# A gated state-space convolution and feed-forward mix on one core: the same steps in another written order

## The chip, the cores and the metric

The kernel runs on one core of one Trainium2 chip. A core has a matrix engine (TensorE, PE in the profile, its weight loads PEld), a vector engine (VectorE, DVE), an engine for functions and scaled copies (ScalarE, ACT), GpSimd (POOL) and SyncE (SP), which here only issues transfers. Each engine takes its instructions strictly in the order in which they were written, and waits on semaphores for what the others made. Matmul results stand in PSUM, everything else in SBUF. The metric is device time in microseconds, the median of three runs; lower is better.

## What is computed

The reference, cut to its core. `x` is 2048 rows of 640, `N` is 128, `F` is 1728:

```python
g = sigmoid((x * gate_w).sum(-1, keepdims=True))
# a: a long convolution of x along the rows, one kernel K for each of 640 columns
P = exp((dt * A)[:, :, None] * arange(L))
K = einsum("dn,dnl,dn->dl", C, P, dt * B).real
a = irfft(rfft(pad(x.T)) * rfft(pad(K))).T + x * Dskip
# b: a gated feed-forward block
b = (gelu(x @ w_gate) * (x @ w_up)) @ w_down
return g * a + (1 - g) * b
```

## The kernel before

Everything is cut into named steps. A dictionary holds for each name a small function that issues one or a few instructions. At the end a loop goes through the words of the table `ORDER` and calls them one after the other; the order in the table is the order on every engine's queue. What follows a slash in a word is either the PSUM buffer of a matmul group (0 to 3; there are four, of two banks each) or the engine of an eviction (A for ACT, D for DVE). Nothing else decides the order.

The names that the text uses, with `.0` and `.1` for the two halves of 320 of the 640 columns in the tables, and of 1024 rows in the feed-forward part:

- `lp0` to `lp5`: loads of the six parameter matrices (A_re, A_im, C_re, C_im, B_re, B_im; line 265); `t0` to `t5` turn them on PE (L297); `al` (L319), `al2` and `th` (L322) are decay and phase on DVE; `c2`, `c3` copy two turned ones on ACT (L326); `v0` to `v18` compute a square root and an angle from them, on DVE and ACT in turn.
- `xa`, `xb`: exponentials on ACT (L447, L449, L457, L461), single (320 wide) and double (640); `tabE`, `tabT`, `tabG`: loads of ACT's function tables.
- `fa`, `fb`: phases on DVE (L469, L477, L464); `sa`, `sb`: their sines on ACT (L481, L487); `ma`, `pa`, `pb`, `pc`: products on DVE (L492, L496, L505). When all of one half are there, `ct` contracts them on PE (L517, L518) in six blocks of 24 matmuls and one of 16, and `ek` copies each block out, in two instructions (L381 or L383). `ks` adds the skip term, `kd` and `kt` send the result out and back in another layout. `oa` and `ob` are memsets on POOL (L545, L546).
- `g`, `u`, `h`: gate and up projections on PE (L376), ten matmuls of 512 each; `eg`, `eu` evict them, `sg`, `su` spill what is kept in DRAM. `lw`, `x`: loads of weights and of the transposed input. `gl`: 80 small matmuls for the gate `g`. For late parts `dg` and `du` evict with the gelu and the product at once.
- `uf`: folds of the input (L367), each from a plain load `ul` and two gathers `ur` on POOL (L360). `us` stores a fold, `lu` loads a part of it.
- `rl`, `rg`: loads of spilled parts; `ge`: gelu on ACT; `hm`: up times gelu on DVE (L682). The loads `rl` share a ring of three slots.
- `U`, `K`: the two transforms on PE (L693, L706), `eU`, `eK` their evictions; `m`, `s`, `y`: products and sums in the frequency domain on DVE (L748 to L755); `I`: the inverse (L766), `eI`; `D`: down projection (28 matmuls, L781); `Z`: the mix (L788, L789); `o` evicts, `st` stores.

The written order runs in stages that overlap: parameters and exponentials (to about 31 us), the first half's tables beside the projections of the first 1024 rows (to 74), the first contraction (74.7 to 80.7), the second half's exponentials (to 98), its tables beside the second rows' projections (to 141), the second contraction, transforms and gelu (to about 184), and products, inverses, down projections and stores to the end.

Of the kernel before, what the change touches and what calls it, by code (L numbers as in the profile page):

```python
# [50 lines left out]
sa4.0 g11.0/0 eg11.0/A sa3.0 lw6 g12.0/1 eg12.0/A su8.0 su9.0 x4.1 us1 su7.0 pa4.0 fa6.0 leu1 ul2 sa6.0 pa3.0 fa5.0
g10.0/3 eg10.0/A sa5.0 pa6.0 ma5.0 pa5.0 u11.0/2 eu11.0/A u10.0/0 u12.0/1 ur2 eu10.0/A ct0.2/3 ct0.1/2 ct0.4/0
eu12.0/A ek0.4/A fb0.1 uf2.0 ek0.2/D uf2.1 ct0.0/1 ct0.6/3 ek0.6/D ek0.1/A ct0.3/0 ct0.5/2 ek0.3/D ek0.0/D ek0.5/D
ks.0 lw7 su10.0 su11.0 h.0/3 eg13.0/D ul3 su12.0 us2 ob.1 ur3 tabE2 xa11.1 xb11.1 xb3.1 xb21.1 xa17.1 xb19.1 xa9.1
xa15.1 xa16.1 eu13.0/D uf3.0 ma5.1 lw8 h.1/0 oa.1 xa7.1 xb23.1 g12.1/1 xa3.1 xa14.1 xa10.1 ma3.1 eg12.1/D xb5.1 xb27.1
xb1.1 xb17.1 xa19.1 xb14.1 xb10.1 xb13.1 xb4.1 xb7.1 xb31.1 xb25.1 xb9.1 xa8.1 xb6.1 xb12.1 xb2.1 xb8.1 xa4.1 xb29.1
xa1.1 xa5.1 xb15.1 tabT2 sb0.1 u12.1/2 eu12.1/D su13.0 eg13.1/D sg13.1 sg12.1 leu3 su12.1 uf3.1 ma2.1 u0.1/3 eu0.1/D
ma6.1 g0.1/1 g1.1/2 kd.0 lw9 eu13.1/A gl/3 gl1 ma4.1 fb1.1 ma1.1 eg0.1/D sg0.1 su0.1 lfm ma0.1 us3 sb1.1 u1.1/1 g2.1/0
lw10 su13.1 fb2.1 pb0.1 pc0.1 pb1.1 pc1.1 sb2.1 U000/3 eg2.1/A eU000/A fb4.1 pb2.1 pc2.1 eg1.1/A eu1.1/A fb3.1 fil.1
sb4.1 sg2.1 u2.1/0 sg1.1 eu2.1/A su1.1 lkm fa0.1 pb4.1 pc4.1 sb3.1 g3.1/3 U001/2 eU001/A u3.1/1 eg3.1/A u4.1/0 U003/2  # L60
fb5.1 pb3.1 pc3.1 lw11 su2.1 sg3.1 sa0.1 pa0.1 fa2.1 g4.1/3 eu3.1/A eU003/A sb5.1 eg4.1/A eu4.1/A su3.1 sa2.1 U002/1
g5.1/2 pb5.1 fa1.1 fa4.1 pa2.1 eg5.1/A sa1.1 u5.1/3 g6.1/0 kt.0 su4.1 sg4.1 eu5.1/A eg6.1/A sg5.1 pa1.1 fa3.1 sa4.1
u6.1/2 eu6.1/A su5.1 sg6.1 lwd0 su6.1 lu01 u7.1/3 K000/0 sa3.1 fa6.1 pa4.1 pa3.1 fa5.1 eU002/A K001/2 eK001/A g7.1/1
K011 eK011/D eu7.1/A sa6.1 eg7.1/D pa6.1 sa5.1 K002/3 K003/2 eK002/A K012 eK003/A K013 pa5.1 eK000/A eK012/A K010
ct1.4/1 ct1.5/3 lw12 lw13 su7.1 rl0.0 tabG sg7.1 eK013/D m0001 ek1.4/D ek1.5/D eK010/A ge1.0 gl2 ct1.2/2 ct1.1/0
ek1.1/A ek1.2/A ct1.3/1 hm0.0 rl3.0 rg3.1 ct1.6/3 ct1.0/0 rl1.0 lkm2 rl2.0 ek1.3/D m0100 ek1.6/A U012/2 eU012/A U013/1
eU013/A U010/3 U011/2 m0000 y000 ek1.0/A ks.1 eU010/D ge3.0 eU011/A gl3 m0110 y001 s0100 hm1.0 g8.1/1 g9.1/0 u9.1/3
K022/2 dg8 ge12.0 dg9 ge13.0 gf/1 gf1 ge9.0 ge5.0 g10.1/0 lu03 kd.1 du9 hm3.0 hm2.0 m0111 m0101 eK022/A K021/1 u8.1/3
g11.1/2 s0101 dg10 u10.1/0 pm0/A ge7.0 ge11.0 dg11 eK021/A rg1.1 rl4.0 hm4.0 lim rl6.0 rg6.1 rl5.0 lu02 er0 rl7.0 du8
y011 hm6.0 hm5.0 rg7.1 rg0.1 rl9.0 rl8.0 du10 y010 u11.1/3 K023/2 eK023/A U033/1 eU033/A hm7.0 du11 U022/0 eU022/A  # L70
U020/2 eU020/A hz0 hz1 lwz0 lwz1 U021/1 eU021/A rl10.0 er1 U023/0 eU023/A K031/3 eK031/A rg5.1 lu10 U031/2 U032/1
eU032/A eU031/A I001/0 K032/3 eI001/A eK032/A I000/1 eI000/A m0211 hm8.0 rl11.0 hm10.0 K033/2 U100/0 eK033/A U030/3
eU100/A eU030/A U103/1 U101/2 eU101/A U102/0 eU102/A eU103/A K020/3 eK020/A I011/2 K030/0 eK030/A m0220 hm9.0 rl13.0
lwe0 m0210 hm11.0 rl12.0 ge1.1 s0220 hm12.0 hm13.0 m0221 s0221 rg4.1 rg2.1 rl0.1 rg13.1 ge13.1 er2 rl1.1 kt.1 lu11
m0200 hm1.1 hm0.1 s0200 m0201 I010/1 m0300 eI010/A s0201 y021 m0310 ge5.1 rl4.1 lu12 rg12.1 rl2.1 D000/3 Z000 o000/A
# [789 lines left out]
```

## Time and profile before

| | us |
|---|---|
| median of 3 runs | 290.28 |
| the three runs | 290.28, 289.33, 291.79 |
| the profiled execution | 288.91 |
| its span, first to last instruction | 287.1 |
| PE, DVE, ACT busy | 264.5, 261.8, 222.7 |

The mean granted clock of the matrix engine was 0.988 of full speed. In the rows of the timeline that are shown, the first number is the start in microseconds from the span's start and the second the duration; then engine, line, operation, what it writes and reads, how many, and in brackets the idle time of the engine ahead of it with what ended it. "SPq" and "POOL" rows on transfers give the time of issuing, not that of the transfer. Matmuls overlap in the array, so the time between starts counts, not the duration of one.

### The profile page before, as it was taken

How to read it: one execution, taken by the hardware profiler on the slowest of the kernel's cores; microseconds unless marked ns; L12 is line 12 of the kernel's file. 1: busy time of each engine (PE TensorE's matmuls, PEld its weight loads, DVE VectorE, ACT ScalarE, POOL GpSimd, SP SyncE). 2: the span in 40 equal slices, each digit the busy share in tenths (PEclk: the TensorE clock that was granted, in tenths of full speed). 3: DMA queues.
4: the chain of work that ended last, by engine and by line, in shares of the span. 5: the costliest groups of instructions: out<-in, count | busy, mean ns of one | idle time of the engine just before them, and what ended most of it. 6: DMA issues, size and time to landing. Idle time of an engine off the chain costs nothing.

```text
span 287.1 us, 4933 instructions
## 1 busy us (share of the span) xinstructions
PE 264.5 (92%) x1883; PEld 159.8 (56%) x1883; DVE 261.8 (91%) x336; ACT 222.7 (78%) x324; POOL 14.1 (5%) x23
## 2 busy tenths in 40 slices
PE   3899799999999699998799998999999999999974
PEld 1744344444754434444584455777777767777753
DVE  1689999999998898999999999999999999999960
ACT  4699999799899978999999988999856545313320
POOL 2202000030040000000010000000000000000000
PEclk9999999999999969999999999999999999999999
DMA  7992479979382897858948877782355000010001
GB/s 200 221 227 75 136 223 272 213 182 304 101 265 66 193 321 220 301 186 263 332 117 222 278 200 215 225 256 67 95 142 162 25 23 23 25 46 25 23 23 46
DMA packets 63148, 46.94 MB, mean 163 GB/s; under 512 B 23275, under 2 KB 53526, under 8 KB 62998
## 3 DMA queue, kind: packets, MB, share of 16 engines
q1 hardware_dynamic: 62166, 44.90, 55.4%
q0 software_dynamic: 384, 1.31, 1.6%
q10 hardware_dynamic: 576, 0.43, 0.5%
q8 instruction: 14, 0.23, 0.3%
q14 instruction: 8, 0.07, 0.1%
HBM read 29.39 MB, written 14.62 MB: 153 GB/s over the span
## 4 chain that ended last, share of the span: by engine, by line
PE 36%; DVE 32%; ACT 17%; DMA 8%; issue 4%; SPq 2%; POOL 0%; DVEq 0%; ACTq 0%
PE ps L376 15%; DVE work L751 8%; DVE work L752 8%; PE ps L781 7%; DVE work L748 5%; PE ps L693 4%; ACT tail L481 3%; DMA work<-PMd 3%; PE ps L766 2%; ACT work L381 2%; ACT tail L487 2%; PE ps L706 2%; DVE work L383 2%; PE ps L517 2%; DMA tail<-PMd 2%
## 5 line engine op out<-in xcount | busy, mean ns | idle before, releaser
L376 PE MATMUL ps<-xT,Wr 128*128 128x512 bf16 x540 | 122.1, 385 | 7.1 <-DVE work L383 3.2
L376 PEld LDWEIGHTS <-Wr 128*128 128x128 bf16 x540 | 53.3, 99 | 72.4 <-issue 12.5
L381 ACT CAST work<-ps 128x640 bf16<-128x640 f32 (+2 forms) x59 | 47.8, 842 | 14.2 <-PE ps L766 7.5
L387 ACT ACTIVATE Wr<-ps,gs 128x320 bf16<-128x320 f32 x29 | 13.7, 524 | 29.4 <-issue 16.4
L752 DVE TENSOR_TENSOR work<-work 128x2560 bf16<-128x2560 bf16 x24 | 35.8, 1490 | 0.7
L781 PE MATMUL ps<-xT,work 128*128 128x320 bf16 x224 | 31.7, 299 | 0.0
L781 PE MATMUL ps<-xT,H 128*128 128x320 bf16 x224 | 31.6, 299 | 0.0
L481 ACT ACTIVATE tail<-work 128x1920 bf16<-128x1920 int16 x14 | 25.7, 1854 | 1.8 <-DVE work L464 1.7
L781 PEld LDWEIGHTS <-H 128*128 128x128 bf16 x224 | 21.9, 98 | 8.5
L781 PEld LDWEIGHTS <-work 128*128 128x128 bf16 x224 | 21.9, 98 | 8.5
L505 DVE TENSOR_TENSOR work<-tail,work 128x1920 bf16<-128x1920 bf16 (+1 forms) x22 | 23.1, 1090 | 0.0
L487 ACT ACTIVATE tail<-work 128x960 bf16<-128x960 int16 (+1 forms) x24 | 20.8, 926 | 0.8 <-DVE work L505 0.8
L766 PE MATMUL ps<-work,tail 128*128 128x320 bf16 x128 | 19.5, 299 | 1.8 <-DVE work L754 1.8
L469 DVE SCALAR_TENSOR_TENSOR work<-tail 128x320 int32<-128x320 f32 x42 | 18.0, 483 | 0.9 <-ACT tail L487 0.5
L464 DVE TENSOR_SCALAR work<-work 128x960 int32<-128x960 int16 (+1 forms) x26 | 16.5, 634 | 1.3
L766 PEld LDWEIGHTS <-tail 128*128 128x128 bf16 x128 | 12.4, 98 | 7.4 <-issue 2.2
L693 PEld LDWEIGHTS <-early 128*128 128x128 bf16 x128 | 12.4, 98 | 7.1 <-DMA tail<-PMd 1.7
L706 PE MATMUL ps<-KTt,early 128*128 128x320 bf16 x80 | 15.0, 299 | 1.4 <-ACT early L387 1.2
L496 DVE TENSOR_TENSOR work<-tail,work 128x1920 bf16<-128x1920 bf16 x14 | 15.9, 1151 | 0.3 <-ACT tail L481 0.3
L383 DVE CAST work<-ps 128x1024 bf16<-128x1024 f32 (+2 forms) x11 | 12.4, 1146 | 2.6 <-PE ps L766 1.6
L457 ACT ACTIVATE work<-tail 128x320 bf16<-128x320 f32 x30 | 12.5, 454 | 1.4 <-DVE tail L319 1.4
L693 PE MATMUL ps<-work,early 128*128 128x320 bf16 x80 | 13.1, 299 | 0.0
(119 smaller groups left out, 405.6 us busy)
## 6 DMA issues: line engine op xcount, KB each, us to landing
Ud<-work SPq DMA_DIRECT2D x22, 256.0 KB
work<-Ud SPq DMA_DIRECT2D x22, 256.0 KB
Wr<-in_B_w_gate_dram SPq DMA_DIRECT2D x12, 320.0 KB
Wr<-in_B_w_up_dram SPq DMA_DIRECT2D x12, 320.0 KB
PMd<-early SPq DMA_DIRECT2D x4, 640.0 KB
Gd<-work SPq DMA_DIRECT2D x9, 256.0 KB
work<-Gd SPq DMA_DIRECT2D x9, 256.0 KB
out_dram<-Wr SPq DMA_DIRECT2D x14, 160.0 KB
```

The source lines that it names most:

```text
L376: P.matmul(t[:, x, :], lhsT=Wr[:, slot, kt, cols:cols + 128], rhs=xT[:, th, kt, 512 * x:512 * x + 512], start=(kt == 0), stop=(kt == 4))
L381: A.copy(out=out, in_=in_)
L383: V.tensor_copy(out=out, in_=in_)
L481: act(out=T, in_=low16(t)[:, :, :, ::2], func=ACT.Sin, scale=SIN_SCALE)
L487: act(out=o[:, r], in_=i[:, r], func=ACT.Sin, scale=SIN_SCALE)
L505: tt(out=B2[:, :, :, cols].rearrange("p r g x -> p g r x"), in0=Tv if hf == 0 else Tv[:, :, ::-1], in1=e, op=ALU.mult)
L693: P.matmul(t[:, r, 0:W2], lhsT=FM[:, e, r, 128 * m:128 * m + 128], rhs=pm[:, r, e], start=(e == 0), stop=(e == 1))
L706: P.matmul(t[:, r, 0:W2], lhsT=mat[:, r, 128 * m:128 * m + 128], rhs=KTt[:, q, d], start=(x == 0 and j != 1), stop=(x == len(seq) - 1), sk ...
L751: step(f"m{h}{c}{i}{part}", lambda ux=ux, kx=kx: tt(out=fl(t), in0=ux, in1=kx, op=ALU.mult))
L752: step(f"s{h}{c}{i}{part}", lambda dst=dst, op=op: tt(out=fl(dst), in0=fl(dst), in1=fl(t), op=op))
L766: P.matmul(t[:, r, 0:W2], lhsT=IM[:, m, r, 128 * e:128 * e + 128], rhs=Y[:, r, m], start=(m == 0), stop=(m == 3))
L781: P.matmul(t[:, x, 0:W2], lhsT=H[c // 2][:, ft, tk:tk + 128], rhs=at[f"Wd{h}"][:, ft], start=(ft == 0), stop=False)
```

## The change

Only the table `ORDER` differs. The 875 words name the same steps; nearly every one stands in another place. The search that had made the first table was carried on, with the figures it works with unchanged. 17 words change the engine of an eviction, and many the PSUM buffer of a matmul group. The first line of the table, of before and of after:

```diff
-ldt leu2 lp3 one oa.0 idx sk ob.0 lp0 lpk tdt/0 t0/1 tabE dt al xb27.0 al2 xa4.0 xb14.0 xb17.0 xb4.0 xb8.0 xa1.0
+lp0 lpk ldt one tdt/0 t0/1 tabE dt al xb21.0 oa.0 sk al2 xb5.0 hz0 idx leu2 lp1 t1/2 xb1.0 xb19.0 xb25.0 xa8.0 xb3.0
```

The words that change engine, in the order of before:

| from DVE to ACT | from ACT to DVE |
|---|---|
| `eg2.0`, `ek0.2`, `eg0.1`, `eg7.1`, `ek1.4`, `ek1.5`, `ek1.3`, `o121` | `eu12.0`, `ek0.4`, `eu13.1`, `eu7.1`, `ek1.2`, `eK010`, `ek1.6`, `o1300`, `o1311` |

Three places are shown on their engines. The first is the head of SP's queue, before; `early` holds the parameters here, `Wr` the projections' weights, `xT` the transposed input:

```order
L261 DMA work<-in_A_log_dt_dram 1x640
L655 DMA edge_u<-in_A_u_dram 3x640
L265 DMA early<-in_A_C_im_dram 128x640
L265 DMA early<-in_A_C_re_dram 128x640
L272 DMA Wr<-in_B_w_gate_dram 128x5x256
L273 DMA Wr<-in_B_w_up_dram 128x5x256
L265 DMA early<-in_A_A_im_dram 128x640
L280 DMA_TRANSPOSE xT<-in_A_u_dram 128x1024
L265 DMA early<-in_A_B_im_dram 128x640
```

And the same place on SP after:

```order
L261 DMA work<-in_A_log_dt_dram 1x640
L655 DMA edge_u<-in_A_u_dram 3x640
L265 DMA early<-in_A_A_im_dram 128x640
L265 DMA early<-in_A_C_im_dram 128x640
L265 DMA early<-in_A_C_re_dram 128x640
L265 DMA early<-in_A_B_im_dram 128x640
L265 DMA early<-in_A_B_re_dram 128x640
L272 DMA Wr<-in_B_w_gate_dram 128x5x256
L273 DMA Wr<-in_B_w_up_dram 128x5x256
L280 DMA_TRANSPOSE xT<-in_A_u_dram 128x1024 x5
```

A_im, from which the phase `th` is made, moved from the seventh place to the third, and all parameters stand ahead of weights and input.

The second place is DVE at the first contraction, before; L496 and L492 are the last table products, L477 with L464 a phase chunk of the other half (`fb0.1`), L367 folds, L383 on `early` the copies `ek`:

```order
L496 TENSOR_TENSOR work<-tail,work 128x3x2x320
L477 TENSOR_SCALAR work<-tail 128x320 x3
L464 TENSOR_SCALAR work<-work 128x960
L367 TENSOR_TENSOR early<-early 128x1280
L383 CAST early<-ps_66 128x84x6 x2
L367 TENSOR_TENSOR early<-early 128x1280
L383 CAST early<-ps_66 128x84x6
L383 CAST early<-ps_66 128x84x2
```

And DVE at the same place after:

```order
L367 TENSOR_TENSOR early<-early 128x1280
L496 TENSOR_TENSOR work<-tail,work 128x3x2x320 x2
L383 CAST early<-ps_64 128x84x6 x2
L367 TENSOR_TENSOR early<-early 128x1280
L383 CAST early<-ps_66 128x84x6 x2
L477 TENSOR_SCALAR work<-tail 128x320 x3
L464 TENSOR_SCALAR work<-work 128x960
```

The phase chunk and the fold `uf2.0` that stood between the last product and the first copy now stand behind the second copy and ahead of the last products.

The third place is POOL, where the gathers (L360, two to a fold) and the memsets `oa.1` (L545) and `ob.1` (L546) stand; as a piece of the difference:

```order
 L546 MEMSET work 128x80x4
 L360 DMA early<-in_A_u_dram,back 128x640 x6
+L545 MEMSET work 128x320
 L546 MEMSET work 128x80x4
 L360 DMA early<-in_A_u_dram,back 128x640 x2
-L545 MEMSET work 128x320
-L597 MEMSET H_78 64x1024
```

Both memsets now stand ahead of the last two gathers, where one stood behind them; the memset of `H` moved to the head.

More of the change, by code (lines that the diff above doesn't have):

```diff
@@ L51 @@
[L51 to L60, printed above, removed]
@@ L71 @@
[L71 to L75, printed above, removed]
@@ new lines @@
+uf2.1 su10.0 ul3 us2 ct0.2/2 ct0.4/3 ek0.4/D su11.0 ct0.3/1 ct0.0/0 ct0.6/3 fb0.1 ek0.0/D ek0.6/D ek0.2/A tabE2
+u12.0/2 eu12.0/D xb23.1 xb29.1 xb25.1 xa4.1 xa3.1 xb12.1 xb15.1 xa5.1 xb10.1 xb8.1 xa9.1 xa14.1 xb9.1 xa16.1 xb3.1
+xb31.1 xb19.1 xa19.1 xb27.1 xa8.1 xa7.1 xb11.1 xb13.1 xa17.1 xb21.1 xa15.1 xa1.1 xb6.1 xb1.1 xb7.1 xa11.1 xa10.1
+xb17.1 xb4.1 xb14.1 xb5.1 xb2.1 tabT2 sb0.1 h.0/0 ek0.3/D oa.1 ob.1 ur3 uf3.0 uf3.1 ks.0 g12.1/3 eg12.1/D eu13.0/D
+fil.1 lw8 kd.0 su12.0 su13.0 sg12.1 fb1.1 ma2.1 eg13.0/D ma4.1 ma6.1 h.1/2 eg13.1/D ma0.1 g1.1/1 u12.1/3 eu13.1/D
@@ new lines @@
+hm11.0 ge12.0 dg9 K030/1 eK030/A hm13.0 u9.1/2 du9 leu0 rl12.0 rg1.1 lwz0 lwz1 lwe0 U032/0 eU032/A hm12.0 ge1.1 ge3.1
+pm0/A I011/3 I010/1 m0211 er2 rl0.1 rl2.1 kt.1 ge12.1 eI010/A pm1/A rl1.1 hm0.1 rl3.1 m0221 hm2.1 s0221 m0200 D000/0
+D001/2 Z001 o001/A Z000 K102/1 eK102/A s0200 m0300 hm1.1 m0201 s0201 y021 y020 o000/A eI011/A ge5.1 ge13.1 pm2/A rl5.1
+rg7.1 rl4.1 rg6.1 ge7.1 st000 lu10 hm3.1 m0310 hm5.1 m0301 hm4.1 s0310 m0311 rl6.1 lu11 rl12.1 D010/2 D011/0 Z010
+o010/A rl7.1 hm6.1 U101/3 eU101/A hm7.1 s0311 hm12.1 rl13.1 st001 st010 Z011 o011/A K112 eK112/A I020/2 eI020/A K121/3
```

69 lines of the change are left out of this document (37 added, 32 removed).

## The prediction

> **What bounds the kernel now.** I read the page first, then the waits, then the timeline of each engine, named against the step list.
>
> ```profile
> span 287.1 us, 4933 instructions
> PE 264.5 (92%) x1883; PEld 159.8 (56%) x1883; DVE 261.8 (91%) x336; ACT 222.7 (78%) x324; POOL 14.1 (5%) x23
> DVE  1689999999998898999999999999999999999960
> ACT  4699999799899978999999988999856545313320
> PEclk9999999999999969999999999999999999999999
> ```
>
> PE and DVE are both full; ACT is full until about 170 us. The place to ask which of them sets the end is the end itself (timeline, last microseconds; columns are start, duration, engine, line, idle before and its releaser):
>
> ```profile
> 275.28 0.82 DVE L754 TENSOR_TENSOR work<-work 128x1280 bf16<-128x1280 bf16 x1
> 276.15 2.33 PE L766 MATMUL ps<-work,tail 128*128 128x320 bf16 x16 [1.77 <-DVE work L754]
> ```
>
> PE waits 1.77 us for `y130`, the last product on DVE, which ends at 276.1; inverse, mix, last down projection, eviction and store follow, 11.0 us to the span's end. Both orders have the same steps behind `y130`, and `D131` stands after it in both, so I keep 11.0. The end is therefore DVE's clock: its start (al, 5.02), its work up to `y130`, and its waits. The waits by releaser, in total, times, longest:
>
> ```profile
> DVE tail L319 <- PE ps L297: 5.0, 1, 5.0
> DVE tail L322 <- PE ps L297: 3.0, 1, 3.0
> DVE work L383 <- DMA Gd<-work: 0.9, 1, 0.9
> DVE early L367 <- DMA early<-in_A_u_dram,back: 0.9, 1, 0.9
> DVE work L339 <- ACT work L338: 0.8, 1, 0.8
> DVE work L469 <- ACT tail L487: 0.5, 1, 0.5
> DVE early L383 <- PE ps L518: 0.4, 1, 0.4
> DVE work L496 <- ACT tail L481: 0.3, 1, 0.3
> DVE work L469 <- ACT tail L481: 0.3, 1, 0.3
> DVE work L343 <- ACT work L341: 0.2, 1, 0.2
> ```
>
> Some 7.3 us of waits behind `al` are all that an order can win, less what it adds. From 126 us on DVE hardly waits, so the second half has nothing to give while PE keeps ahead of it.
>
> **The change, term by term.** No step is added or removed; I sum what DVE waits, before and after.
>
> *1, the head.*
>
> ```profile
> 3.37 0.52 SPq L265 DMA_DIRECT2D early<-in_A_A_im_dram  x1
> 8.11 5.81 PE L297 MATMUL ps<-picks,early 128*128 128x64 bf16 x50 [3.20 <-DMA early<-in_A_A_im_dram]
> 5.88 0.47 ACT L457 ACTIVATE work<-tail 128x320 bf16<-128x320 f32 x1 [1.41 <-DVE tail L319]
> 14.20 0.46 ACT L447 ACTIVATE work<-tail 128x320 bf16<-128x320 f32 x1
> 14.56 0.73 ACT L449 ACTIVATE work<-tail 128x640 bf16<-128x640 f32 x1
> 15.19 0.46 ACT L447 ACTIVATE work<-tail 128x320 bf16<-128x320 f32 x1
> 8.68 5.45 SPq L280 DMA_TRANSPOSE xT<-in_A_u_dram  x4
> DMA to landing us min/median/max: 3.1/4.2/4.6
> ```
>
> A_im is issued at 3.37 behind 640 KB of weights and holds `th` back. Now it is SP's third transfer instead of its seventh, and all parameters go ahead of the weights; `th` follows `al2` at 6.3 at once, so the 3.0 goes. What is late next is `c2` on ACT: ahead of it now stand six single exponentials (0.36 from start to start), five double ones (0.63) and `c3` (0.7), 6.0 us from 5.88, so `c2` runs to 12.5. DVE has two phase chunks of 1.4 and two products of 0.73 after `th` and is at `c2`'s reader `v0` at 11.4: a new wait of 1.1. Then the first fold (`uf0`) now stands ahead of `v8`. Its load follows five transposes on SP (1.36 each, so about 12.5), its second gather the turns on PE (about 12); with the 4.2 of the gather row it lands at about 16.3, DVE is there at 15.4: 0.8 to 1.3, I take 1.1; with it `v8` no longer waits. `v12` waits about 0.3. After 2.5, before 3.0 + 0.8 + 0.2 = 4.0: **-1.5**. Were the parameters no earlier it would be +1.5; were both new waits covered, -3.7.
>
> *2, the first contraction.*
>
> ```profile
> L517 PE MATMUL ps<-work x80: 198/200/201, 74.7 to 80.6; 128*128 128x84 bf16 x80
> 79.05 4.60 DVE L383 CAST early<-ps 128x504 bf16<-128x504 f32 x8 [0.41 <-PE ps L518]
> ```
>
> 160 matmuls in 6.0 us make 0.9 us for a block of 24. Before, DVE had `fb0.1` and `uf2.0` to do while PE filled the first banks, and waited 0.41 later. Now `ek0.5` comes right behind the last product, and it reads the second block: 2 x 0.9 + 0.1 = 1.9 us with nothing under it. Against 0.3 + 0.4: **+1.2**. It is zero at best (if PE ran ahead, which it can't: the block needs the last product), 1.9 at worst.
>
> *3, the last fold.*
>
> ```profile
> 80.90 0.36 POOL L546 MEMSET work<- 128x320 bf16 x1 [18.25 <-PE ps L518]
> 82.91 0.95 POOL L360 DMA_INDIRECT early<-in_A_u_dram,back  x1 [0.30 <-issue]
> 87.36 0.82 DVE L367 TENSOR_TENSOR early<-early 128x1280 bf16<-128x1280 bf16 x1 [0.86 <-DMA early<-in_A_u_dram,back]
> ```
>
> Before, one memset, two gathers and 4.45 us from the second gather's start to `uf3.0`. Now two memsets stand ahead of the gathers, and all wait for the end of the contraction, 6.0 after its start S: second gather at S + 8.5, data at S + 12.95. DVE reaches `uf3.0` at S + 11.1 (1.9, then five pairs of copies at 1.2 each, one short by 0.2, `uf2.1` 0.74, `fb0.1` 1.4, `eu12.0` 1.2). Wait 1.85 against 0.86: **+1.0**, bounds -0.9 (hidden) and +1.2 (at 4.6). [...]
>
> *4, the bare stretch on PE.* ACT makes 37 exponentials here and empties no bank. Windows (PE, PEld, DVE, ACT, POOL busy, clock, DMA):
>
> ```profile
> 91.40:95.70 4.30, 4.30 (x21) 1.96 (x20) 3.18 (x5) 4.30 (x11) 0.00 (x0) 1.00 0.38 113
> 95.70:99.10 3.40, 2.36 (x82) 2.07 (x80) 3.37 (x8) 3.38 (x7) 0.00 (x0) 1.00 0.90 186
> 99.10:102.50 3.40, 1.64 (x4) 0.56 (x4) 3.29 (x8) 3.34 (x6) 0.00 (x0) 0.50 0.93 275
> 102.50:105.90 3.40, 3.40 (x9) 1.21 (x8) 3.40 (x4) 2.62 (x3) 0.00 (x0) 0.50 1.02 288
> 100.86 6.97 PE L376 MATMUL ps<-xT,Wr 128*128 128x512 bf16 x20 [2.09 <-DVE work L383]
> ```
>
> For 5.1 us PE does little but the 80 small matmuls of `gl`; then the clock is 0.50 for 6.8 us, and 20 matmuls take 6.97 where they take 4.3. After, with DVE's copies placed as they are, `u12.1` ends at S + 19.0, `gl` runs S + 21.0 to 23.1 and `u0.1` starts at S + 25.1: 6.1 us with little but `gl`. At full clock `eu0.1` on DVE finds it 0.65 done ahead; at half it costs DVE 1.5, and if `g0.1` falls under it too, 1.4 more through ACT. Bounds 0 and 2.9; I take half of the first step, 0.75, and 0.3 for the later waits of this stage on ACT (that row's smaller entry). Before: 0.9 + 0.2 + 0.5 + 0.3 = 1.9. **-0.85**.
>
> [...]
>
> *5, ring loads.*
>
> ```profile
> 210.48 3.56 DMA work<-PMd
> 173.09 5.17 DMA tail<-PMd
> 173.99 1.38 DVE L682 TENSOR_TENSOR H<-H,work 128x1024 bf16<-128x1024 bf16 x2
> 181.16 1.28 DVE L682 TENSOR_TENSOR H<-H,work 128x1024 bf16<-128x1024 bf16 x2
> 152.36 4.03 SPq L533 DMA_DIRECT2D Kd<-tail  x4
> ```
>
> `rl13.0` can go once `hm10.0` has freed its slot. Before, it took 6.4 us from there to `hm13.0` (174.7, the second of the first row, to 181.8), now 2.65 (two more `hm`, one `s`). A load takes 3.56 to 5.17 in these nearest rows (of 320 KB; this one has 128): wait 0 to 2.8, I take **+0.5**.
>
> *6, work.* Of the copies that change engine most pair off. DVE loses three pairs of the second contraction's copies (3.6) and gets two others, one short (2.2), and one 128x640 copy (0.8): **-0.6**; `o121` leaves and two last evictions come behind `y130`, where DVE idles.
>
> PE, which must stay ahead for this to hold: `u12.0` (2.2) moves behind the contraction, so PE gets there no later than the products do. `D000` can start with `hm12.0`, which by DVE's rows stands 94.7 us ahead of `y130`; from there PE has 92.6 to do to `I130` (90.3 before, and `U100` to `U103`, 2.2, that stood ahead of `D000`). It has 2 us to spare, as it had 1.77: nothing.
>
> Sum: -1.5 + 1.2 + 1.0 - 0.85 + 0.5 - 0.6 = -0.25. The profiled execution took 288.91 us (span 287.1 and 1.8 around it), 1.37 below the median of 290.28. 288.91 - 0.25 = 288.7, and on the median's scale 290.0.
>
> **Rivals.** *Faster: the gather lands at its minimum.* With 3.1 for 4.45, `uf3.0` waits 0.5 (-1.35), `gl` comes earlier, the bare stretch is 4.7, under the 5.1 that cost the clock (-0.75), and the ring loads, halves of the rows' size, are hidden (-0.5): -2.85 against the median, 287.4. It decides where the gather takes under 3.5. For it: the row's 3.1. Against: the one landing at this place was 4.45.
>
> *Slower: the half clock holds over two groups.* `u0.1` and `g0.1` both at half, as `u1.1` and `g2.1` were: DVE loses 2.9 for my 0.75, sum +1.9: 292.2. It decides once the stretch holds the drop ahead of `u0.1`. For it: 6.1 against 5.1 us. Against: `g0.1` may start in a restored window.
>
> *Slower: SP's queue starves the products.* `rl2.0` now stands behind `kd.1` (the 4.03 us of issue in the row above), and `hm2.0`, `hm9.0`, `hm13.0`, `hm0.1` each come close behind their loads; at 1.2 each (3.56 + 0.3 - 2.65, with 0.3 to issue) it is 4.8 for my 0.5, sum +4.05: 294.3. Against: loads before never showed as a DVE wait. It decides where a ring load takes over 3.
>
> *No change at all* is the forecast's neighbour: term 6 alone gives 289.7.
>
> **How the numbers follow.** A measurement of this kernel tells about 1% from no change (its three runs span 289.33 to 291.79): 287.4 to 293.2. Forecast 0.53, gather 0.22, clock 0.15, ring 0.10. The first rival sits on the upper edge of faster, and better in half of the head's bounds: 0.16 of its 0.22 count as faster, and 0.04 of the forecast. Slower: 0.08 of ring, 0.04 of clock, 0.03 of the forecast. Faster 0.20, same 0.65, slower 0.15. The range leaves out about a tenth on each side: 286.5 to 293.2.
>
> **What would show it.** Right: no wait of `th`; `v0` behind ACT; 1.9 ahead of `ek0.5`; 1 to 2 at `uf3.0` for the gather; a half clock near 95 to 103; DVE full behind 126; PE 1 to 3 idle ahead of the last inverse. Wrong: DVE waits of over 1 us behind 140, PE late for products in the second half, or `y130` more than 3 us from 275.9.

## The result and the profile after

| | kernel before | changed kernel |
|---|---|---|
| median, us | 290.44 (20 runs, 289.30 to 291.79) | 292.53 (20 runs, 291.08 to 297.27) |
| ratio to before | 1 | 1.0074, 95% interval 1.0053 to 1.0094 |
| profiled execution, us | 288.91 | 292.49 |
| its span and mean granted clock | 287.1, 0.988 | 290.7, 0.965 |
| end of `y130` in it | 276.1 | 278.04 |
| from there to the span's end | 11.0 | 12.7 |

The changed kernel is slower by 0.7%: 2.1 us in the medians, 3.6 in the two profiled executions. That is inside the range and inside 1%, but on the other side of the small gain that was forecast. In the profiled executions `y130` comes 1.9 later and the stretch behind it is 1.7 longer. The profiled execution of the kernel before lies 1.5 below its median, that of the changed kernel on its median, so the rows explain 3.6 us where the medians differ by 2.1.

The page of the changed kernel, with the lines that answer to those of before:

```profile
span 290.7 us, 4930 instructions
PE 266.3 (92%) x1869; PEld 160.5 (55%) x1883; DVE 260.8 (90%) x335; ACT 223.0 (77%) x325; POOL 16.2 (6%) x23
DVE  3869999999689989998999999999999999999941
...
PEclk9859999999999689999999999999999999999979
```

DVE has lost 1 us of work and is still the engine that sets the time. The clock was under full speed in three places, where before it was in one (0.50 from 99.1 to 105.9): 0.50 from 11.9 to 22.1 us, 0.50 from 97.3 to 104.1, and 0.50 from 278.2 to 281.6.

The waits of DVE by releaser (total, times, longest):

```profile
DVE tail L319 <- PE ps L297: 4.8, 1, 4.8
...
DVE early L367 <- DMA early<-in_A_u_dram: 2.8, 1, 2.8
DVE early L383 <- PE ps L518: 2.2, 1, 2.2
DVE work L496 <- ACT tail L481: 1.8, 2, 1.2
DVE work L383 <- PE ps L376: 1.6, 1, 1.6
DVE early L367 <- DMA early<-in_A_u_dram,back: 1.0, 1, 1.0
DVE work L331 <- ACT early L326: 1.0, 1, 1.0
```

The wait of `th` (L322, 3.0) is gone and nearly every line below it is new: the first fold for its plain load, the first copy of the contraction for its block, two products for late sines, the first projection behind the gate.

The end of the changed kernel, in the timeline of DVE and of PE:

```profile
277.22 0.82 DVE L754 TENSOR_TENSOR work<-work 128x1280 bf16<-128x1280 bf16 x1
278.10 4.02 PE L766 MATMUL ps<-work,tail 128*128 128x320 bf16 x16 [2.59 <-DVE work L754]
```

The last inverse takes 4.02 us where it took 2.33. The windows around it (duration, then PE, PEld, DVE, ACT, POOL busy, granted clock, DMA share, rate) say why:

```profile
274.80:278.20 3.40, 0.81 (x7) 0.40 (x5) 3.17 (x4) 0.00 (x0) 0.00 (x0) 1.00 0.23 71
278.20:281.60 3.40, 3.40 (x14) 1.93 (x14) 0.00 (x0) 0.69 (x1) 0.00 (x0) 0.50 0.00 0
```

PE is ahead and has 0.81 us of work in the first window; in the second it is full, at a granted clock of 0.50. That is the 1.7 behind `y130`.

### The profile page after: what moved, and what is told of

It is laid out like the page before. It is cut to its first block, busy times and chain, and to the rows that moved or that the text cites. A ratio compares the mean times of both kernels' runs of the same rounds, so it can differ in the third digit from the quotient of the medians.

```text
span 290.7 us, 4930 instructions
## 1 busy us (share of the span) xinstructions
PE 266.3 (92%) x1869; PEld 160.5 (55%) x1883; DVE 260.8 (90%) x335; ACT 223.0 (77%) x325; POOL 16.2 (6%) x23
## 4 chain that ended last, share of the span: by engine, by line
DVE 54%; issue 16%; ACT 8%; PE 8%; DMA 6%; SPq 6%; POOL 0%; DVEq 0%; ACTq 0%; POOLq 0%
DVE work L751 11%; DVE work L752 11%; DVE work L748 6%; PE ps L376 4%; DVE work L505 3%; SPq L280 3%; DVE work L383 3%; DVE H L682 3%; ACT work L381 2%; DVE work L755 2%; DVE work L754 2%; DVE work L464 2%; DMA Gd<-work 2%; DMA work<-Ud 2%; DVE work L492 1%
## 5 line engine op out<-in xcount | busy, mean ns | idle before, releaser
L376 PE MATMUL ps<-xT,Wr 128*128 128x512 bf16 x526 | 123.5, 389 | 11.9 <-DMA xT<-in_A_u_dram 4.1
L381 ACT CAST work<-ps 128x640 bf16<-128x640 f32 (+1 forms) x58 | 46.6, 842 | 19.2 <-PE ps L766 8.6
L766 PE MATMUL ps<-work,tail 128*128 128x320 bf16 x128 | 21.0, 317 | 2.8 <-DVE work L754 2.8
L383 DVE CAST work<-ps 128x1024 bf16<-128x1024 f32 (+2 forms) x12 | 13.8, 1152 | 5.8 <-PE ps L766 4.1
L766 PEld LDWEIGHTS <-tail 128*128 128x128 bf16 x128 | 13.1, 103 | 9.4 <-DVE work L754 3.4
L496 DVE TENSOR_TENSOR work<-tail,work 128x1920 bf16<-128x1920 bf16 x14 | 16.1, 1153 | 1.9 <-ACT tail L481 1.8
L464 DVE TENSOR_SCALAR work<-work 128x960 int32<-128x960 int16 (+1 forms) x26 | 16.5, 634 | 1.4
L693 PEld LDWEIGHTS <-early 128*128 128x128 bf16 x128 | 12.7, 99 | 6.1 <-DMA early<-fm_c 0.3
L387 ACT ACTIVATE work<-ps 128x640 bf16<-128x640 f32 x16 | 11.2, 713 | 4.2 <-PE ps L706 3.4
```

The lines of the kernel that those rows point to most:

```text
L376: P.matmul(t[:, x, :], lhsT=Wr[:, slot, kt, cols:cols + 128], rhs=xT[:, th, kt, 512 * x:512 * x + 512], start=(kt == 0), stop=(kt == 4))
L381: A.copy(out=out, in_=in_)
L383: V.tensor_copy(out=out, in_=in_)
L387: act(out=out, in_=in_, func=ACT.Copy, scale=scale)
L464: ts(out=t[:, 1, 0:n], in0=low16(t[:, 0, 0:n])[:, :, ::2], scalar1=TURN / 4, scalar2=None, op0=ALU.add)
L766: P.matmul(t[:, r, 0:W2], lhsT=IM[:, m, r, 128 * e:128 * e + 128], rhs=Y[:, r, m], start=(m == 0), stop=(m == 3))
```

## The experiments

All are edits of the changed kernel, unless said otherwise, each timed in five rounds (the last repeat in one) beside the kernel before on the same chip. Ratios are to the kernel before; an edit's own effect is read against 1.0074, at 2.9 us for 0.01. The edits worth about 1 us have intervals that overlap the changed kernel's, so their sizes are rough; what they did is read from the traces. In the cuts of code `...` stands for words left out, and counts are written out in place of their names.

### The stretch behind `y130`

**Matmuls that fill PE's wait.**

```diff
+                    if job == "I130":
+                        for _ in range(12):
+                            P.matmul(t[:, 0, :], lhsT=IM[:, 0, 0, 0:128], rhs=H[1][:, 0, 0:512], start=True, stop=True)
```

> The changed kernel with 12 matmuls of 128x512 added on PE ahead of the last inverse; their result is overwritten by it and nothing else is left out. Theory (the 2.59 us that PE waits for y130 drop the clock to 0.50 for the last inverse, whose two groups then take 4.02 instead of 2.33 each way): the row of 278.2 to 281.6 goes to 1.00, the stretch behind y130 falls from 12.7 to about 11.0, the time by 1.7 to about 290.8 (ratio to the kernel before about 1.002). y130 itself stays where it is, at 278.0. Rival (the stretch behind y130 is longer because other steps stand in it): the clock rises and the stretch stays over 12.3, time 292.5 or, where the fillers run into y130's end, up to 1 us more.

Measured: 290.96, ratio 1.0038 (1.0016 to 1.0060), 1.0 less than the changed kernel. The timeline and the window:

```profile
278.10 2.33 PE L770 MATMUL ps<-work,tail 128*128 128x320 bf16 x16
...
278.20:281.60 3.40, 3.40 (x26) 2.44 (x25) 1.13 (x2) 0.69 (x1) 0.00 (x0) 1.00 0.02 5
```

Same `y130`, a clock of 1.00 for 0.50, 2.33 for the inverse, 10.9 behind `y130` (289.0 - 278.05). The cause of the longer stretch is shown: the half clock. In the median it costs about 1.0 and not 1.7, and it doesn't come in every execution: of the eight profiles with this same idle time ahead of the inverse (the changed kernel and seven of its edits), three have the inverse at 2.35 and one at 3.51. The first row is of the run with the load moved, the second of that with the store moved, both described below:

```profile
280.06 2.35 PE L766 MATMUL ps<-work,tail 128*128 128x320 bf16 x16 [2.58 <-DVE work L754]
...
276.31 3.51 PE L766 MATMUL ps<-work,tail 128*128 128x320 bf16 x16 [2.59 <-DVE work L754]
```

So the same 2.6 us of idle stands once ahead of 4.02 and once of 2.35; what decides between the two was not shown.

**Useful work in that wait.**

```diff
-y131 y130 I130/1 eI130/A I131/0 Z130 D131/3 eI131/D
+y131 y130 D131/3 I130/1 eI130/A I131/0 Z130 eI131/D
```

> The changed kernel with one step moved: D131 (last down projection of the other half, 40 matmuls of about 0.1 us) written ahead of I130, so that it runs while PE waits for y130. Theory (clock): PE's idle ahead of the inverse falls from 2.6 to under 1, the clock stays at 1.00, and the stretch behind y130 loses the 1.7 of the half clock and a part of D131's own time that stood in it, 12.7 to between 9.5 and 11: time 289 to 291. Rival (the clock drop costs nothing, the chain behind y130 is DVE's and ACT's): at most the time of D131, 0 to -1, time 291.5 to 292.5.

Measured: 288.93, ratio 0.9971 (0.9948 to 0.9993): 3.0 less than the changed kernel, by one word.

```profile
280.41 2.34 PE L766 MATMUL ps<-work,tail 128*128 128x320 bf16 x16
```

`D131` (28 matmuls, not the 40 of the expectation, 0.14 from start to start: 3.9 us) ends 1.1 after `y130` (279.30), so the inverse starts that much later, but at a clock of 1.00 (the window of 278.2 to 281.6) and with this down projection done: 8.8 us from `y130` to the end.

**The same in the kernel before.**

```diff
-Z121 o121/D I130/3 I131/0 eI130/A Z130 eI131/D D131/1 Z131
+Z121 o121/A D131/1 I130/3 I131/0 eI130/A Z130 eI131/D Z131
```

> The kernel before with D131 written ahead of I130 (and the eviction o121 on ACT). Theory (in the kernel before too PE's wait of 1.77 for y130 is bare, and D131's 40 matmuls stand in the 11.0 us behind y130): the stretch behind y130 falls to 9, the time by about 2, ratio to the kernel before 0.993. Rival (the chain behind y130 is set by evictions and the store): ratio 0.998 to 1.002.

Measured: 290.17, ratio 1.0016 (0.9993 to 1.0040). The theory missed; the timeline of PE says where:

```profile
276.76 3.96 PE L781 MATMUL ps<-xT,work 128*128 128x320 bf16 x28 [1.08 <-ACT Wr L387]
280.56 1.66 PE L766 MATMUL ps<-work,tail 128*128 128x320 bf16 x11
```

There PE has less time ahead of `y130`, and `D131` waits 1.08 for an eviction by ACT first, that of `o121`, which this edit had moved to ACT. It ends 3.2 after `y130` (277.39); the stretch behind is 10.9, as before. So the place ahead of the inverse won 3.0 in the changed order and nothing in this one, where PE is less far ahead.

### The head

**The fold's load ahead of the transposes.**

```diff
-lw0 x3.0 x0.0 v2 v1 ... leu3 ul0 uf0.1
+lw0 ul0 x3.0 x0.0 v2 v1 ... leu3 uf0.1
```

> The changed kernel with one transfer moved: the plain load of the first fold (ul0) ahead of the five transposes on SP. Theory (the head gave nothing because this load waits behind transposes of 1.92 us each): the wait of the first fold on DVE falls from 2.8 to under 1, y130 comes 1.5 to 2 earlier, time about 290.8. Rival 1 (the transposes come 0.5 later, the projections behind them with them, and the gain turns into a wait of the first copies out of the banks): y130 moves by less than 0.5, time 292 to 293. Rival 2 (the gather lands as late as the load): the wait stays over 2.

Measured: 292.28, ratio 1.0080 (1.0050 to 1.0111): no gain. First the rows of the changed kernel, then those of this one, from the timelines of SP, POOL and DVE:

```profile
4.79 9.60 SPq L280 DMA_TRANSPOSE xT<-in_A_u_dram  x5
...
15.03 0.39 SPq L356 DMA_DIRECT2D early<-in_A_u_dram  x1
...
18.31 1.56 DVE L367 TENSOR_TENSOR early<-early 128x1280 bf16<-128x1280 bf16 x2 [2.80 <-DMA early<-in_A_u_dram]
```

```profile
10.90 1.12 POOL L360 DMA_INDIRECT early<-in_A_u_dram,back  x1 [7.44 <-PE ps L297]
12.32 0.95 POOL L360 DMA_INDIRECT early<-in_A_u_dram,back  x1 [0.30 <-issue]
...
19.13 1.56 DVE L367 TENSOR_TENSOR early<-early 128x1280 bf16<-128x1280 bf16 x2 [3.00 <-DMA early<-in_A_u_dram,back]
```

Rival 2 holds: the fold waits 3.00. In the changed kernel the five transposes hold SP for 9.60 us (1.92 each; the forecast used 1.36), and the load goes out at 15.03. With the load ahead of them, the gathers are the last to land: the second is issued at 12.32 and its data is used at 19.13, 6.8 later, where the forecast had 4.2. Rival 1 shows too: the projections start again at 19.66 for 16.92, and the copy `eu0.0` now waits 1.40 for them.

**The fold later.**

```diff
-ul0 uf0.1 uf0.0 ur1 us0 u0.0/3 ... v10 eu0.0/D xb8.0
+ul0 u0.0/3 ... v10 eu0.0/D uf0.1 uf0.0 ur1 us0 xb8.0
```

> The changed kernel with the first fold (uf0, its store and the next gathers) put back behind the first copy out of a bank (eu0.0), about where the kernel before has it. Theory (the gain of the head was given back in DVE's wait of 2.7 to 4.1 for the fold's transfers, and there is other work to cover it): the wait falls under 0.5, v8 and the copy wait 0 to 1 in its place, y130 comes 1.5 to 2.5 earlier, time 290 to 291. Rival (the steps ahead wait as long, for ACT's exponentials or for the projections behind the transposes): the sum of the head's waits stays within 0.7 of the changed kernel's, time 292 to 293.

Measured: 295.15, ratio 1.0177 (1.0139 to 1.0215), 3 us more, above the ranges of the theory and of the rival. **The same, and matmuls that keep PE busy in the head:**

```diff
+                if job == "u0.0" and x == 0 and kt < 2:
+                    for _ in range((12, 18)[kt]):
+                        P.matmul(t[:, 1, :], lhsT=H[0][64:128, 13, 0:128], rhs=H[0][64:128, 13, 0:512], start=True, stop=True)
```

> The kernel with the first fold later (the run before) and 12 and 18 matmuls of 128x512 added on PE around the first matmul of u0.0, where PE stood idle from 9.1 to 18.4; they go into the bank half that u0.0 overwrites. Theory (PE's idle in the head, which the earlier parameters make, drops the clock, and the first group at half clock holds DVE's eu0.0 for 4.0): clock 1.00 from 12 to 22, the wait of eu0.0 2.0 or less, y130 2 earlier, time 292.5 to 293.5. Rival (the last transpose sets when u0.0 can run, and the clock adds little): the wait stays over 3, time 294.3 to 295.5.

Measured: 295.80, ratio 1.0205 (1.0175 to 1.0236). The copy `eu0.0` in DVE's timeline, without and with the added matmuls:

```profile
21.97 1.22 DVE L383 CAST work<-ps 128x1024 bf16<-128x1024 f32 x1 [4.04 <-PE ps L376]
```

```profile
19.81 1.23 DVE L387 CAST work<-ps 128x1024 bf16<-128x1024 f32 x1 [1.57 <-PE ps L380]
```

The fold no longer waits, but the copy behind it then waits 4.04 for the first projection, whose input comes with the last transpose and which runs at half clock: PE stood idle for 3.55 and 5.13 us around its first matmul, and the clock was 0.50 from 11.9 to 20.4. With the added matmuls the clock is 1.00 from 1.0 to 24.0 and the wait 1.57, as expected. Some 1.4 of the difference is the clock's (the copy starts 2.14 behind the last input for 3.57); the input also came 0.7 earlier in that profile (17.67 for 18.40), and DVE 0.3 later. The time is not better all the same (the intervals overlap, and that profile has a new wait of 1.4 for a ring load). So the clock's part of this one wait is shown, its price in the time is not. The 3 us of the later fold stand in its waits: 2.3 more in the head than in the changed kernel (0.97 + 1.04 + 4.04 for 0.97 + 2.80), 0.6 at the second fold's load and 0.3 at the last fold.

**One parameter earlier, in the kernel before.**

```diff
-ldt leu2 lp3 one ... lp2 lw0 lp1 x0.0
+ldt leu2 lp1 lp3 one ... lp2 lw0 x0.0
```

> The kernel before with one transfer moved: A_im (lp1) as SP's third instead of its seventh, everything else as it was. Theory (the head's end is set by the queue of transfers behind, so a wait won at its start comes back): th waits 0, and v3, v0 or v8 wait 2 to 3 in its place; ratio 0.998 to 1.003. Term 1 as predicted (the wait of 3.0 goes and little comes back): y130 1.5 to 3 earlier, ratio 0.990 to 0.995.

Measured: 290.11, ratio 0.9996 (0.9975 to 1.0017). In the timeline of DVE and of PE:

```profile
6.30 0.82 DVE L322 SCALAR_TENSOR_TENSOR tail<-ps,early 128x640 f32<-128x640 f32 x1
...
13.21 0.82 DVE L334 TENSOR_TENSOR work<-ps,early 128x640 f32<-128x640 f32 x1 [3.17 <-ACT early L326]
...
10.13 4.05 PE L297 MATMUL ps<-picks,early 128*128 128x64 bf16 x40 [4.15 <-DMA early<-in_A_B_im_dram]
```

This is the first half of term 1 by itself (A_im earlier, the other parameters where they were), and it is worth nothing: `th` no longer waits 3.02, and `v3`, two phase chunks behind it, waits 3.17, since B_im goes out at 6.99, behind a transpose that holds SP for 3.10.

### The first contraction

```diff
-ct0.5/1 ek0.5/D uf2.1 ... ct0.6/3 fb0.1 ek0.0/D
+ct0.5/1 fb0.1 ek0.5/D uf2.1 ... ct0.6/3 ek0.0/D
```

> The changed kernel with one step moved: the 1.4 us phase chunk fb0.1 ahead of ek0.5, so that DVE has work while PE fills the first banks of the contraction. Theory (the wait of 2.2 is bare since nothing stands under it, as term 2 has it): the wait falls to about 0.8, y130 comes 1.4 earlier less what the last fold then waits more (up to 1.2, since DVE gets to it sooner and its gathers do not), time 291 to 292. Rival (the banks are emptied later and PE's contraction with them): y130 moves by less than 0.3, time 292.3 to 292.8.

Measured: 293.55, ratio 1.0108 (1.0065 to 1.0150); the interval reaches the changed kernel's. DVE's timeline, of the changed kernel:

```profile
76.10 1.27 DVE L383 CAST early<-ps 128x504 bf16<-128x504 f32 x2 [2.22 <-PE ps L518]
...
86.00 1.56 DVE L367 TENSOR_TENSOR early<-early 128x1280 bf16<-128x1280 bf16 x2 [1.00 <-DMA early<-in_A_u_dram,back]
```

and of this one:

```profile
76.37 1.27 DVE L383 CAST early<-ps 128x504 bf16<-128x504 f32 x2 [0.81 <-PE ps L518]
...
79.99 2.10 DVE L383 CAST early<-ps 128x504 bf16<-128x504 f32 x4 [0.43 <-PE ps L518]
82.73 1.22 DVE L383 CAST work<-ps 128x1024 bf16<-128x1024 f32 x1 [0.64 <-issue]
...
86.10 1.56 DVE L367 TENSOR_TENSOR early<-early 128x1280 bf16<-128x1280 bf16 x2 [0.97 <-DMA early<-in_A_u_dram,back]
```

The wait falls from 2.22 to 0.81, as expected, and 0.43 and 0.64 come back within six microseconds. The fold stands at 86.10 for 86.00, and `y130` ends at 278.22 for 278.04, as the rival has it. Nothing is won: the gathers, which wait for the end of the contraction, are issued at the same time (the second at 82.63 for 82.70), and the fold waits for them. So terms 2 and 3 are one chain, and were summed as two.

### The stretch with little on PE

**Matmuls behind the gate.**

```diff
+        for _ in range(16):
+            P.matmul(t[:, 1, :], lhsT=xT[:, 0, 0, 0:128], rhs=xT[:, 0, 0, 0:512], start=True, stop=True)
```

> The changed kernel with 16 matmuls of 128x512 behind the gate's 80 small ones, into a bank half that nobody reads; nothing is left out. Theory (the small matmuls count as idle, the stretch drops the clock, and the half clock behind it makes DVE wait 1.56 for the first group at 102.8 and makes the spill behind it late): no row at 0.50 from 97 to 104, that wait under 0.4, y130 0.7 to 1.5 earlier, time 291 to 291.8. Rival (PE has slack there, and the waits come from the banks and the ring, not the clock): the clock is 1.00, the waits stay within 0.4 of theirs, time 292.3 to 293.5 (the fillers' 3.5 us may even add).

Measured: 291.21, ratio 1.0025 (0.9993 to 1.0058), 1.4 less than the changed kernel. Windows of the changed kernel, then of this one:

```profile
93.90:97.30 3.40, 2.14 (x80) 2.07 (x80) 3.37 (x6) 3.40 (x9) 0.00 (x0) 1.00 0.80 211
97.30:100.70 3.40, 2.14 (x5) 0.84 (x6) 3.37 (x5) 3.24 (x4) 0.00 (x0) 0.50 0.61 165
100.70:104.10 3.40, 3.15 (x10) 1.20 (x9) 1.84 (x3) 1.78 (x2) 0.00 (x0) 0.50 0.85 336
```

```profile
97.30:100.70 3.40, 3.40 (x31) 1.71 (x29) 3.37 (x5) 3.37 (x6) 0.00 (x0) 1.00 0.64 152
100.70:104.10 3.40, 3.17 (x17) 1.46 (x15) 2.55 (x4) 2.19 (x3) 0.00 (x0) 1.00 0.80 295
```

The 80 small matmuls make PE busy for 2.14 of 3.40 us and the clock falls to 0.50 all the same; with 16 wide matmuls behind them it stays at 1.00 here. The waits behind it shrink: `eu0.1` 1.56 to 0.82 (under 0.4 was expected), `pa3.1` 1.24 to 0.33. In this profile `y130` is not earlier (278.02 for 278.04): DVE starts 0.56 later in it and waits 1.0 more for the first fold, so the gain stands in the median and in the waits behind the gate.

**A store ahead of three loads.**

```diff
-su2.1 su3.1 lu01 lwd0 lw11 sg3.1 eK001/A
+su2.1 su3.1 sg3.1 lu01 lwd0 lw11 eK001/A
```

> The changed kernel with one transfer moved: the store sg3.1 ahead of three loads on SP (lu01, lwd0, lw11). Theory (ACT's eu4.1 waits 1.78 for the slot that this store frees, and DVE's pa3.1 1.24 and pa6.1 0.54 wait for what ACT then does late): ACT's wait goes, pa3.1 waits under 0.5, y130 0.7 to 1.2 earlier, time 291.2 to 291.8. Rival (ACT is late from the half clock at 97 to 104, not from the slot): the wait on the store goes and pa3.1 still waits over 0.9, time 292.3 to 292.7.

Measured: 290.77, ratio 1.0037 (1.0013 to 1.0061), 1.1 less. In the changed kernel ACT's copy `eu4.1` and DVE's products:

```profile
131.30 1.01 ACT L381 CAST work<-ps 128x1024 bf16<-128x1024 f32 x1 [1.78 <-DMA Gd<-work]
...
134.05 1.16 DVE L496 TENSOR_TENSOR work<-tail,work 128x1920 bf16<-128x1920 bf16 x1 [1.24 <-ACT tail L481]
...
142.46 1.16 DVE L496 TENSOR_TENSOR work<-tail,work 128x1920 bf16<-128x1920 bf16 x1 [0.54 <-ACT tail L481]
```

and the same copy here, with the store on SP that it had waited for:

```profile
120.36 0.42 SPq L403 DMA_DIRECT2D Gd<-work  x1
...
129.15 1.12 ACT L381 CAST work<-ps 128x1024 bf16<-128x1024 f32 x1
```

No DVE wait on L496 is left, though `eu0.1` still waits 1.6 for its group, as in the changed kernel. The 1.78 on the copy and the 1.78 on the two products come from the store's place: it freed a slot, stood behind loads that wait for other things, and went out at 126 for 120.4. The lateness behind the half clock adds to it: with the store in its old place and the clock at 1.00 behind the gate, in the run before, `pa3.1` waited only 0.33. So what the two edits win can't simply be added.

**The matmuls in the kernel before.**

> The kernel before with 16 matmuls of 128x512 behind the gate's small ones, as in the run on the changed kernel. Theory (the kernel before paid less for its half clock, 1.9 of waits behind it in all, most of them not from the clock): y130 0.3 to 0.8 earlier, ratio to the kernel before 0.997 to 0.999. Rival (both orders pay the same for the half clock): ratio 0.993 to 0.996, as the changed kernel's 1.4 would have it.

Measured: 292.04, ratio 1.0059 (1.0039 to 1.0079): neither. The clock still falls (0.70 from 98 to 100, 0.50 to 102, 0.95 to 104), for a shorter time than without them (0.50 from 100 to 104, 0.68 to 107), and the products `hm` wait for ring loads, 2.0 in two waits that the kernel before hardly has:

```profile
DVE work L685 <- DMA work<-Ud: 1.1, 1, 1.1
...
DVE H L685 <- DMA work<-Ud: 0.9, 1, 0.9
```

It tells nothing on the clock's price in that order; it shows that added matmuls can cost more than they hide.

### Head against rest

**The old head, the changed rest** (the order of before up to `eu11.0` and `u10.0`, then the changed one).

> The order of the kernel before for everything up to u10.0 and eu11.0 (about 73 us), and the changed order for the rest. Theory (the head of the changed order gave nothing, since what th no longer waits is waited for at the fold's transfers): within 0.7 of the changed kernel, ratio 1.005 to 1.010. Rival 1 (term 1 was right and the gain was lost elsewhere): 1.5 slower than the changed kernel, ratio over 1.011. Rival 2 (the changed head costs something, by its half clock): ratio under 1.004.

Measured: 294.09, ratio 1.0140 (1.0107 to 1.0173), slower than the changed kernel by 0.7%, in the range of rival 1. The trace doesn't show rival 1's cause. The last product ahead of the contraction ends 0.80 later than in the changed kernel (74.68 for 73.88), the fold behind the contraction stands 1.81 later (87.81 for 86.00), and `y130` 2.0. The 1.0 in between is made at the seam. There PE, with `u12.0` behind the contraction, has nothing to do for 2.81 us; the clock falls inside the contraction, which takes 7.6 us (74.73 to 82.33) for 6.0. From PE's timeline and the windows:

```profile
74.73 0.20 PE L517 MATMUL ps<-work 128*128 128x84 bf16 x1 [2.81 <-DVE work L496]
...
76.20:79.60 3.40, 3.40 (x66) 3.40 (x64) 1.59 (x3) 1.45 (x3) 0.00 (x0) 0.66 0.22 78
```

Some 0.8 can be the head's; how much of it the contraction would have hidden is not shown.

**The changed head, the old rest.**

> The changed order up to pa5.0 (about 73 us) and the order of the kernel before for the rest; the counterpart of the run with the old head. From the traces so far the changed head takes 0.2 off DVE's start, 0.25 off its waits and about 1.2 of copies off DVE. Theory (so the head is worth 1.5 to 2, by copies and not by waits, and the loss is in the rest): time 288.0 to 288.8, ratio to the kernel before 0.993 to 0.997. Rival (the parts are not additive: what DVE wins ahead of the contraction it waits for there, since the first contraction and the gathers behind it have a time of their own): ratio 0.998 to 1.003.

Measured: 292.30, ratio 1.0053 (1.0024 to 1.0082), above both ranges. Its profiled execution took 296.43, with a wait of 5.61 for the first fold's load, so the rows below are of a second run of the same kernel.

> The changed head on the old rest once more, for its profile: the first one took 4 us more than the median of its runs. Theory (what the changed head wins ahead of the contraction is waited for there): DVE's waits for the banks of the contraction (L383 behind L518) add up to 2 or more, against 0.4 in the kernel before, and y130 lies between 276 and 278. Rival (the head itself waits longer than in the kernel before, for the first fold's load): that load's wait is over 4 and the contraction's waits are under 1.

Measured: 293.17 in two runs, ratio 1.0132 (1.0090 to 1.0175). DVE's timeline at the contraction:

```profile
78.66 1.27 DVE L383 CAST early<-ps 128x504 bf16<-128x504 f32 x2 [2.60 <-PE ps L518]
...
81.89 4.60 DVE L383 CAST early<-ps 128x504 bf16<-128x504 f32 x8 [1.23 <-PE ps L518]
```

3.8 of waits against 0.41 in the kernel before, as the theory has it, but not for its reason, and `y130` (279.83) is later than it said. DVE ends the last product no earlier than in the kernel before (74.66 for 74.60); all its lead is the fold `uf2.0`, which is done by then. PE comes to the contraction later, at 77.49 for 74.65, with `u12.0` just ahead of it, while DVE stands ready from 76.1. This too is the seam's, and the two halves don't add up. What the changed head is worth by itself stays open.

### Together

**Store, `D131` and matmuls.**

> The changed kernel with three edits of the earlier runs together: D131 ahead of I130, the store sg3.1 ahead of three loads on SP, and 16 matmuls of 128x512 behind the gate's small ones into a bank half that nobody reads. Theory (the three places are independent, and each gave in the medians 3.0, 1.1 and 1.4 from 291.9): 286.4, ratio to the kernel before 0.986 to 0.991. Rival (spill and clock are one wait, ACT being late for both reasons and the second cause taking over when one goes): only the larger of the two counts, 287.5, ratio 0.991 to 0.995.

Measured: 287.56, ratio 0.9905 (0.9879 to 0.9931): the ratio of the theory, the time of the rival. **Store and `D131` alone**, two moved words:

> The changed kernel with D131 ahead of I130 and the store sg3.1 ahead of three loads, without added matmuls. Theory (in the run with all three edits the added matmuls bought nothing, since its clock was 0.50 behind the gate all the same): as that run, 287.3 to 288.0, ratio 0.989 to 0.992. Rival (they hid part of the half clock): 288.3 to 289.0, ratio 0.994 to 0.997.

Measured: 287.23, ratio 0.9884 (0.9855 to 0.9913): 1.2% faster than the kernel before and 1.9% faster than the changed one. That is 5.5 us where the two edits gave 3.0 and 1.1 singly; the intervals together are about as wide as the 1.4 between. The added matmuls bought nothing here: 16 of them took 5.30 us, where they took 3.61 in the run with them alone, with the clock at 1.00. DVE's waits in the last one, behind the start:

```profile
DVE early L367 <- DMA early<-in_A_u_dram: 3.8, 1, 3.8
DVE early L383 <- PE ps L518: 2.2, 1, 2.2
DVE work L383 <- PE ps L376: 1.6, 1, 1.6
```

The wait on L496 is gone, the last inverse takes 2.34 and the end is 8.7 long (278.38 for the inverse's start, 277.27 for the end of `y130`); the head and the contraction stand as in the changed kernel.

## Why the forecast was wrong, by its steps

| term | forecast | by the rows |
|---|---|---|
| DVE's start | 0 | -0.2 |
| 1, the head's waits | -1.5 | -0.2 (0.97 + 2.80 for 3.98) |
| 2, the first contraction | +1.2 | +1.5 (2.22 for 0.41 + 0.29) |
| 3, the last fold | +1.0 | +0.1 (1.00 for 0.86) |
| 4, the stretch with little on PE | -0.85 | +1.4 (1.56 + 1.24 + 0.54 for 1.9) |
| 5, ring loads | +0.5 | +0.2 |
| 6, work (what is left) | -0.6 | -0.9 |
| `y130` | -0.25 | +1.9 |
| behind `y130` | 0 | +1.7 in the profile, 1.0 in the median |

**Term 4 failed by most.** The mechanism was right (a longer stretch, 5.2 us for 5.1, a clock of 0.50 behind it, `eu0.1` late by 1.56) and so was the first step's 1.5, of which only half was taken; but "0.3 for the later waits of this stage on ACT" was carried over from a row of before, and measured 1.78. Those waits come from a store that the new order puts behind three loads on SP: with the store ahead of them they are gone, and the time is 1.1 less. I had followed SP's queue for what loads do to the products, and not for a store that frees a slot on ACT's side. The third rival had the right queue with the wrong transfer; the ring loads cost 0.2.

**"I keep 11.0" failed.** The same steps stand behind `y130`, and `D131` stands after it in both orders, but the wait ahead of it grew from 1.77 to 2.59, and with 0.8 more of idle the inverse ran at half clock and took 4.02 for 2.33. I had written that PE would be idle 1 to 3 us there and had seen a clock of 0.50 behind a stretch with little on PE in another place (99.1 to 105.9 in the kernel before), and didn't put the two together. Nor are the 7.3 of waits behind `al` all that an order can win, as the prediction says: `D131` ahead of the inverse shortens the stretch behind `y130` to 8.8.

**Term 1 failed by its size.** `th` did come at once, and `v0` waited 0.97 behind ACT for 1.1 forecast. The fold behind it waited 2.80 for 1.1, because the transposes were taken at 1.36 from the kernel before and took 1.92 here, so that the load went out at 15.03 for 12.5. With the load ahead of them the gathers, taken at 4.2, hold the fold as long. The fold's wait is 2.2 to 4.1 in the other profiles with this head, and once 5.6, so this term is known to about 1 us. The run with A_im alone earlier shows the same in the kernel before: a wait taken away at the head's start comes back behind it. Nor had I seen that PE, with its turns done by 9.4 and the input late, would stand idle in the head; its row in the changed kernel, in a stretch where the clock was 0.50 from 11.9 to 22.1:

```profile
16.92 1.87 PE L376 MATMUL ps<-xT,Wr 128*128 128x512 bf16 x4 [4.08 <-DMA xT<-in_A_u_dram]
```

**Terms 2 and 3** are near in sum (+2.2, measured +1.6), and the 1.9 that nothing covers is right (2.22). Term 3 alone is not: the last fold waits 1.00 for 1.85, since its second gather, forecast well (74.03 + 8.5), was used 3.30 after its start and not 4.45:

```profile
82.70 0.95 POOL L360 DMA_INDIRECT early<-in_A_u_dram,back  x1 [0.30 <-issue]
```

The two were not independent, as the run with the phase chunk shows.

**Term 6** was right in sign and near in size (DVE's busy time up to `y130` is 0.95 less). PE did stay ahead for the second half, as forecast, and ahead by more.

**The rivals.** The first one's condition came true, a gather under 3.5, and its time didn't: the fold still waited 1.00 for 0.5, PE's stretch with little but `gl` was 5.2 us (93.16 to 98.34) for 4.7, and the clock fell to 0.50. The slower one with the half clock over two groups named 292.2, which is nearly the time that came, but not by its mechanism: `eu0.1` alone was late by the clock, and `g0.1` was not.

**The signs.** All that was to show the forecast right did come (`th`, `v0`, 2.22 ahead of `ek0.5`, 1.00 at `uf3.0`, the clock near 97 to 104, 2.59 ahead of the last inverse) but one: behind 126 DVE still waited 1.24 and 0.54 on L496. And `y130` came 1.9 later with none of the signs of wrong; they were too coarse to see this change.

What stays open is what the half clock behind the gate costs in the kernel before, and what the changed head is worth by itself. A head in which the transposes don't stand behind the weights was not tried.

## What to carry to other kernels

Moving one load forward in the head's queue won nothing here in two tries (ratio 0.9996 with A_im alone earlier in the kernel before, 1.0080 for 1.0074 with the fold's load ahead of the transposes); ask what stands in line behind it, and price it by what the queue's transfers take in their new neighbourhood, not in the old one (1.92 us a transpose here, for 1.36). Where an order puts an engine further ahead, look at once what the longer idle does to its clock (2.59 us of it for 1.77, and an inverse of 4.02 for 2.33 in the changed kernel's profile), and whether a step that now stands behind can fill it: here one word was worth 3 us. Follow stores as well as loads through a queue: here ACT waited 1.78 for a store that frees a slot, which went out at 126 for 120.4.

## What the runs showed of the hardware

- With 2.58 or 2.59 us of idle ahead of it, the last inverse took 3.88 to 4.02 us in four of eight profiles, 3.51 in a fifth and 2.35 in three; with 1.77 or 1.78 it took 2.33 in all of five. In the changed kernel, where PE was busy for 0.81 us of the 3.40 ahead of it, the granted clock was 0.50 from 278.2 to 281.6. Behind 80 matmuls of one column, busy for 2.14 of 3.40 us, it was 0.50 as well (97.3 to 104.1).
- Five transposing transfers issued in a row behind 640 KB of weights held SP for 9.60 us in the changed kernel (1.92 each), 8.92 with matmuls added in the head (1.78) and 8.08 with the fold's load ahead of them (1.62), where four in the kernel before took 5.45 (1.36); the wait of the first fold behind them was between 2.2 and 4.1 in the profiles of the kernels with the changed head and the fold in its place, and 5.6 in the execution that took 296.43.
